# A new front for a fused attention and feed-forward kernel: log sums by a scan, zero matmuls ahead of the first scores, a first-layer group in quarters, and chunk 0's second layer by pairs of tiles

## The chip, the core and the metric

The kernel runs on one core of a Trainium2 chip. The metric is the device time of one execution in microseconds (us). Before the change the median of three runs is 324.0 us (323.47 to 324.17). Engines are named as in the profile: PE is TensorE (matmuls), PEld its weight loads, DVE is VectorE, ACT is ScalarE, POOL is GpSimd and SP is SyncE. Engines run side by side, each through its own instructions in order, and wait for one another by semaphores.

## The reference

```python
# attention with a forget gate; B=8, H=8, S=576, D=64
scores = (q @ k.T) / sqrt(D)
cum    = cumsum(log(clip(f, 1e-4, 1)))           # along the sequence
scores = where(causal, -1e9, scores + cum[:, None] - cum[None, :])
x      = softmax(scores) @ v                      # (B, H, S, D) -> (B*S, H*D) = (4608, 512)
# feed-forward
out    = gelu_tanh(x @ w_in) @ w_out              # w_in 512 x 2048, w_out 2048 x 512
```

## The kernel before

**Attention.** Four heads are one "quad", so there are 16 quads, two for each batch. `q` and `k` of a quad come by a casting DMA on POOL's queue and are put into column layout by a DVE transpose each (`TQ`, `TK`). Scores are computed with the keys on the partitions: a matmul with 32 rows per head, four heads side by side in four 32-row strips of the array (`S`; `H` does two heads only). ACT takes the exponential from PSUM into `pt` (line 285). The triangle at the diagonal is cut off afterwards, by POOL (`M`, line 291) or by DVE with a 0/1 mask (`m`, line 321). The decay needs no term in the scores: the factor exp(-cum - 64) of each key goes into the weights. `wT` holds it, `w_bf` is its bf16 copy, and `vw` is v times it (`vw` on DVE, `VW` on POOL). Denominators (`D`) and outputs (`V`) are matmuls with 32 columns per head, four heads side by side in four 32-column strips. DVE turns a denominator into a factor with transpose, reciprocal, transpose, and multiplies it into `xT` (line 379), which is the feed-forward input, transposed.

**Feed-forward.** Rows go in chunks of 512. The first layer multiplies `w_in` by `xT` with the whole array; ACT applies the gelu into `gT`. For chunk 0 it is done in halves of 256 rows and groups of four 128-wide blocks of d_ff: `J.half.group` (line 419). Groups with a capital J use the pool `psS` (two buffers of two PSUM banks, shared with the scores); those with a small j use the single tile of `psO`, shared with D and V. The second layer of chunk 0 (`mlp_out`, lines 658 to 674) computes four tiles of 128 rows, each as 16 "pulls" of 512 columns; a pull with the capital letter (`F.0.n`, n pulls) uses the whole array, one with the small letter (`f.0.n`) does the same in four strips of 32 columns. Later chunks use seven products in place of eight (`seven_products`, `F.c`/`f.c`, 256 columns a pull), with sums of the weights (`U`) and of the gelus (`G`) made on DVE.

**What sets the order.** The whole program is written out by hand in tables of words: `FRONT` up to the end of batch 3's attention and most of chunk 1's second layer, then `SECOND`, `STEADY` and so on, one word being one step. Each engine gets its instructions in the order of the words. So a step that waits holds up everything behind it on its engine. DMA words (`WI` and `WO` for the weights, `LQ`, `LK`, and `LP`, `LC` for v) stand in POOL's queue among the POOL masks; `LV` and the output stores stand in SP's.

**The front.** `setup` loads `f`, clips it (line 694) and takes its logarithm on ACT (695), transposes it on PE by five matmuls in FP32 into `ps_lt` (700), and ACT copies that to `logfT`. `CW` then makes the running sums on PE with FP32 matmuls against a triangle and a matrix of ones (719, 721), behind the first scores, and ACT turns them into `wT`. `B.n.c` are n matmuls of zeros with c columns (line 256) whose result nobody reads.

Of the kernel before, what the change touches and what calls it, by code (L numbers as in the profile page):

```python
# [16 lines left out]
def kernel(  # L17
# [194 lines left out]
    def transpose_words(src, dst):  # L212

        return nc.vector.transpose(  # L214
            out=dst.rearrange("p s c -> p (s c)").bitcast(FP32)
                .rearrange("p (t a) -> p a t", a=S // 32),
            in_=src.rearrange("p a d -> p (a d)").bitcast(FP32)
                .rearrange("p (a d) -> p a d", d=D // 2),
        )
# [33 lines left out]
    def keep_busy(n, cols=512):  # L253

        for _ in range(n):
            nc.tensor.matmul(idle_ps[0][:, 0:cols], idle[:, 0:128], idle[:, 0:cols],  # L256
                             start=True, stop=True)

# [146 lines left out]

    later = {}

    def mlp_in_half(half, g, spare=False):

        if spare:  # L410
            ph = psO.tile([128, 1024], FP32, name="ps_h", tag="po").rearrange("p (a n) -> p a n", n=512)
        else:
            ph = psS.tile([128, 2, 512], FP32, name="ps_h", tag="s")
        n0 = QA * half
        for dts in (range(N_DT - 1), range(N_DT - 1, N_DT)):
            for j in range(4):
                ft = 4 * g + j
                for dt in dts:
# [7 lines left out]
        later[half, g] = lambda: nc.scalar.activation(gT[:, 4 * g:4 * g + 4, n0:n0 + QA],  # L426
                             ph.rearrange("p a (b n) -> p (a b) n", n=QA), AF.Gelu_apprx_tanh)
        if not spare:
            later[half, g]()

# [227 lines left out]
    def mlp_out(c):  # L658

        for n in range(CH // 128):  # L660
            r0 = CH * c + 128 * n
            st = ostage_pool.tile([128, D_MODEL], FP32, name="o_st", tag="o")
            pso = psM.tile([128, D_MODEL], FP32, name="pso", tag="m")
            for ft in range(N_FT):
                cols = 32 if by_columns else 128
                for c0 in range(0, 128, cols):
                    nc.tensor.matmul(pso[c0:c0 + cols, :],  # L667
                                     gT[:, ft, 128 * n + c0:128 * n + c0 + cols],
                                     w_out_sb[:, ft, :],
                                     start=(ft == 0), stop=(ft == N_FT - 1), skip_group_check=True)  # L670
                if ft == N_FT - 1:
                    nc.vector.tensor_copy(st, pso)
                    nc.sync.dma_start(out=out[r0:r0 + 128, :], in_=st)
                yield


    def setup():
        nc.sync.dma_start(out=f_sb, in_=f.rearrange("b h s -> (b h) s"))
        dmas["LK.0"] = load_one(k, k_c, 0)
        dmas["LQ.0"] = load_one(q, q_c, 0)  # L680
        make_identity(nc, ident_f32)
        dmas["LK.1"] = load_one(k, k_c, 1)
        dmas["LQ.1"] = load_one(q, q_c, 1)
        make_upper_triangular(nc, utri_f32, val=1.0, diag=True)
# [9 lines left out]
        nc.vector.tensor_scalar(f_sb, f_sb, 1e-4, 1.0, op0=ALU.max, op1=ALU.min)
        nc.scalar.activation(f_sb, f_sb, AF.Ln)
# [20 lines left out]

    def make_w():
        cum_ps = psM.tile([128, NT * BH], FP32, name="cum_ps", tag="m")
        nc.tensor.matmul(cum_ps, utri_f32, logfT, start=True, stop=True)
# [34 lines left out]
    ops = {
        "W": lambda: cast_w(nc.vector.tensor_copy),
        "w": lambda: cast_w(nc.scalar.copy),
        "CW": make_w,
        "Z": zeros,
        "TR": lambda: triangles(nc.vector.tensor_copy),
# [99 lines left out]
```

## Time and profile before

| | us |
|---|---|
| median of three runs | 324.0 |
| the profiled execution, time | 323.22 |
| the profiled execution, span from first to last instruction | 321.4 |
| PE busy | 309.6 (96% of the span) |
| DVE busy | 242.0 (75%) |
| ACT busy | 212.7 (66%) |
| POOL busy | 107.8 (34%) |

The profile is of one execution. A row of a timeline gives the start, the length, the engine and line, the operation, the tile written and the tiles read, the shape and the count of instructions merged into it; in square brackets stands the idle time before it and what ended it. A matmul's end is modelled and lies past the start of the next one, so what a block of matmuls costs is read from its start to the start of the next block. A row of a list of waits gives the total, the number and the longest wait.

### The profile page before, as it was taken

The page shows a single profiled execution, that of the slowest core. Times are in us where ns is not written, and L with a number is a line of the kernel's source. Part 1 is how long each engine was busy: PE and PEld are TensorE (multiplying, and loading weights), DVE is VectorE, ACT ScalarE, POOL GpSimd, SP SyncE. Part 2 cuts the span into 40 slices and gives each one's busy share as a digit, 9 for nine tenths or more (in the row PEclk, how much of TensorE's full clock was granted, in tenths as well). Part 3 has the DMA queues.
Part 4 walks back from the last instruction along what each step waited for, and adds up shares of the span by engine and source line. Part 5 has one row for each costly group of instructions (what it writes and reads, how often), then busy time and mean ns, then how long its engine had stood idle before and what let it go on. Part 6 is the DMA issues. An engine that isn't in the chain of part 4 may idle for free.

```text
span 321.4 us, 11820 instructions
## 1 busy us (share of the span) xinstructions
PE 309.6 (96%) x5339; PEld 220.7 (69%) x5339; DVE 242.0 (75%) x374; ACT 212.7 (66%) x242; POOL 107.8 (34%) x145
## 2 busy tenths in 40 slices
PE   0899999999999999999999999999999999999996
PEld 0557844544776567776788878767776786688785
DVE  4765337898979879779877987699876866597674
ACT  4676576775766776878767866787586744836610
POOL 8989343522301416400851075205610140000000
PEclk9999999999999999999999999999999999999999
DMA  7999999585126931593139411971011111010203
GB/s 126 218 210 208 247 213 199 104 155 109 35 43 129 227 78 37 116 209 72 39 82 228 87 39 35 190 172 36 7 47 53 37 34 37 30 37 0 100 33 99
DMA packets 47490, 33.41 MB, mean 104 GB/s; under 512 B 29776, under 2 KB 42192, under 8 KB 47440
## 3 DMA queue, kind: packets, MB, share of 16 engines
q0 software_dynamic: 9632, 15.99, 28.3%
q1 hardware_dynamic: 37664, 16.60, 19.1%
q8 instruction: 41, 0.67, 0.9%
q14 instruction: 9, 0.07, 0.1%
q10 hardware_dynamic: 144, 0.07, 0.1%
HBM read 36.85 MB, written 9.44 MB: 144 GB/s over the span
## 4 chain that ended last, share of the span: by engine, by line
PE 91%; ACT 3%; DVE 3%; DMA 2%; issue 1%; POOL 0%; DVEq 0%; POOLq 0%
PE ps_w L600 30%; PE ps_h L395 19%; PE ps_s L277 9%; PE po L347 9%; PE ps_q L520 8%; PE pso L667 4%; PE ps_h L419 4%; PE ps_u L468 4%; DMA q_c<-in_q_dram 2%; PE po_m L333 1%; ACT pt L285 1%; ACT gT L403 1%; DVE xT L379 1%; PE idle_ps L256 1%; PE cum_ps L721 1%
## 5 line engine op out<-in xcount | busy, mean ns | idle before, releaser
L285 ACT ACTIVATE pt<-ps_s 128x1024 bf16<-128x1024 f32 (+2 forms) x100 | 94.0, 990 | 38.6 <-PE ps_s L277 35.9
L291 POOL TENSOR_SCALAR_AFFINE_SELECT pt<-pt 128x512 bf16<-128x512 bf16 (+3 forms) x65 | 41.4, 647 | 95.2 <-ACT pt L285 72.3
L395 PE MATMUL ps_h<-xT,w_in_sb 128*128 128x512 bf16 (+1 forms) x320 | 66.8, 358 | 0.3 <-ACT gT L403 0.2
L395 PEld LDWEIGHTS <-w_in_sb 128*128 128x128 bf16 x320 | 31.2, 98 | 26.6 <-issue 0.6
L600 PEld LDWEIGHTS <-gT 128*32 128x32 bf16 (+1 forms) x1216 | 44.1, 97 | 5.5 <-issue 2.2
L403 ACT ACTIVATE gT<-ps_h 128x1024 bf16<-128x1024 f32 x34 | 34.6, 1017 | 18.7 <-PE ps_h L395 18.4
L600 PE MATMUL ps_w<-w_out_sb,gT 128*32 128x256 bf16 (+1 forms) x1008 | 42.6, 273 | 0.0
L277 PE MATMUL ps_s<-qT,kT 32*128 32x64 bf16 (+5 forms) x896 | 36.3, 263 | 3.2 <-DVE qT L214 3.0
L600 PEld LDWEIGHTS <-gsum 128*32 128x32 bf16 (+1 forms) x948 | 35.4, 97 | 3.8 <-issue 1.5
L231 POOL TENSOR_TENSOR vw<-v_nat,wT 128x1280 bf16<-128x1280 f32 (+1 forms) x13 | 29.6, 2279 | 11.7 <-DMA v_nat<-in_v_dram 11.4
L536 DVE TENSOR_TENSOR usnap<-ps_q,usnap 128x1024 f32<-128x1024 f32 x15 | 17.9, 1222 | 18.6 <-PE ps_q L520 13.2
L277 PEld LDWEIGHTS <-kT 32*128 32x128 bf16 x896 | 16.5, 93 | 19.6 <-issue 10.1
L600 PE MATMUL ps_w<-usum,gsum 128*32 128x256 bf16 (+1 forms) x791 | 30.0, 273 | 0.0
L617 DVE COPY snap<-ps_w 128x512 f32<-128x512 f32 x32 | 21.8, 681 | 6.2 <-PE ps_w L600 6.0
L531 ACT ACTIVATE gT<-usnap 128x1024 bf16<-128x1024 f32 x15 | 15.8, 1054 | 12.1 <-DVE usnap L536 11.8
L379 DVE TENSOR_TENSOR xT<-po,rb 128x576 bf16<-128x576 f32 x26 | 19.5, 752 | 5.6 <-PE po L347 5.3
L347 PE MATMUL po<-pt,vw 128*32 128x64 bf16 (+4 forms) x624 | 22.4, 278 | 0.0
L214 DVE STREAM_TRANSPOSE qT<-q_c 128x576 f32<-128x576 f32 x16 | 19.8, 1246 | 1.7 <-DMA q_c<-in_q_dram 1.7
L347 PEld LDWEIGHTS <-vw 128*32 128x32 bf16 x672 | 14.6, 97 | 9.4 <-issue 2.8
L214 DVE STREAM_TRANSPOSE kT<-k_c 128x576 f32<-128x576 f32 x16 | 19.5, 1246 | 1.9 <-DMA k_c<-in_k_dram 1.9
L208 POOL DMA_DIRECT2D k_c<-in_k_dram x16 | 9.1, 568 | 33.6 <-DVE kT L214 18.0
L520 PEld LDWEIGHTS <-w_in_sb 128*128 128x128 bf16 x160 | 15.6, 98 | 2.5 <-issue 0.4
(135 smaller groups left out, 478.5 us busy)
## 6 DMA issues: line engine op xcount, KB each, us to landing
out_dram<-o_st SPq DMA_DIRECT2D x35, 256.0 KB, 2.3
k_c<-in_k_dram POOLq DMA_DIRECT2D x16, 288.0 KB, 5.3
q_c<-in_q_dram POOLq DMA_DIRECT2D x16, 288.0 KB, 6.3
v_nat<-in_v_dram SPq DMA_DIRECT2D x16, 256.0 KB, 5.4
v_nat<-in_v_dram SPq DMA_DIRECT2D x20, 128.0 KB, 5.1
v_nat<-in_v_dram POOLq DMA_DIRECT2D x8, 256.0 KB, 8.1
w_in_sb<-in_moe_w_in_dram POOLq DMA_DIRECT2D x8, 256.0 KB, 7.8
w_out_sb<-in_moe_w_out_dram POOLq DMA_DIRECT2D x4, 512.0 KB, 11.3
```

Source lines behind the costliest of these rows:

```text
L214: return nc.vector.transpose(out=dst.rearrange("p s c -> p (s c)").bitcast(FP32) .rearrange("p (t a) -> p a t", a=S // 32), in_=src.rearra ...
L231: return eng.tensor_mul(vw[i % 2][:, t0:t1], vb[:, t0:t1, h0:h0 + 4, :], wT[:, i, t0:t1, :].unsqueeze(3).to_broadcast([128, t1 - t0, 4, D]))
L277: nc.tensor.matmul(tiles[h // 2][:, h % 2, c0:c0 + nq], key_columns(i, key, h, c), qq[32 * h:32 * h + 32, q0:q0 + nq, c], start=(c == 0 an ...
L285: nc.scalar.activation(p[:, 2 * g:2 * g + 2, off:off + n], t[:, :, 0:n], AF.Exp, scale=scale)
L291: nc.gpsimd.affine_select(out=x, in_=x, compare_op=ALU.is_ge, fill=0.0, base=0, pattern=pattern, channel_multiplier=-1)
L347: nc.tensor.matmul(po[r0:r0 + w.shape[-1], 448 + q0:448 + q0 + nq], w, p[:, h, col:col + nq], start=(key in (0, "low")), stop=(key in ("lo ...
L379: nc.vector.tensor_mul(xT[:, 2 * u + x, r0 + s0:r0 + s1], po, rbs[i, part])
L395: nc.tensor.matmul(ph[:, j, n * cols:(n + 1) * cols], w_in_sb[:, dt, 128 * ft:128 * ft + 128], xT[:, dt, h0:h0 + cols], start=(dt == 0 and ...
L403: nc.scalar.activation(gelus(c, 2 * pr, 2), ph, AF.Gelu_apprx_tanh)
L520: nc.tensor.matmul(ps[:, k, HC * n:HC * n + HC], w[:, d, 128 * n:128 * n + 128], x[:, d, :], start=(first and n == 0 and d == 0), stop=(d ...
L600: nc.tensor.matmul(ps[c0:c0 + width, n, cols[0]:cols[1]], x[:, j, 128 * n + c0:128 * n + c0 + width], w[:, j, cols[0]:cols[1]], start=(fir ...
L617: copy(kept[name], ps)
```

## The change

- **Log sums.** The transposes of the logarithms, the copies to `logfT` and the FP32 matmuls go. DVE makes the running sum by one scan over the 576 columns (`SC`), PE transposes the sums (`CT`, five matmuls), and ACT makes `wT` from them in two parts (`CE.1`, then `CE.0` for the first two quads). `w_bf` is cast in two parts (`W.0`, `W.1`).
- **Zero matmuls.** 16 of them (7,808 columns) now stand ahead of the first scores, four of those held until the first `TK` (`BK` reads `kT`, and two plain ones are queued behind it); 16 (5,888 columns) stand behind. Before, ten (3,968 columns) stood behind the first scores.
- **Order of the front.** POOL's memsets (`zeros`) go to DVE. The first mask `M.0.0` now stands in POOL's queue ahead of six of the eight loads of `w_in`; before, five stood behind it. The triangle is made later on POOL (`UT`) and cast on ACT (`tr`). Two score rounds of four heads (`S.0.2`, `S.1.2`) become two rounds of two heads each.
- **A first-layer group in pieces.** Group 0 of half 0 is begun with four matmuls over the first quad's two blocks of `xT`, and ended with four and eight more; its sums are copied by DVE from `psO` into `u1` (`RJ`), which frees `psO` for group 1 (two pieces of eight matmuls). The gelu of group 0 is taken later from `u1`.
- **Chunk 0's second layer.** Two tiles of 128 rows are computed together, four pulls of the one and four of the other in turn, so that both buffers of `psM` are held and a quarter of `w_out` serves eight pulls.
- **Behind that**, plain and strip pulls, masks (more of them on POOL), `vw.5`, one sum of weights and the small copies `cl` are put elsewhere. The tables from `SECOND` on are the same, and both fronts end with 97 pulls of chunk 1 done.

```diff
     FRONT = """
-        Z TQ.0 LP.2 TR WI.1 TQ.1 S.0.0 B.1.384 CW WI.0 TK.1 S.0.2 LP.4 LP.3 B.1.512 vw.0.0 B.2.512 H.1.0.1 H.1.1.1 WI.3 M.0.0 W vw.1.0 WI.2 B.2.512
-        WI.5 LQ.2 WI.4 H.1.0.0 D.0.0 M.1.0.1 M.1.0.0 H.0.1.1 V.0.0.0 H.0.1.0 M.0.1 WI.6 V.0.1.0 B.2.256 H.1.1.0 B.1.256 D.1.0 H.0.3.0 B.1.256 V.1.0.0 H.0.3.1
-        WI.7 LK.2 V.1.1.0 m.0.3.2 H.1.3.0 j.0.0 vw.0.1 H.1.3.1 LC.1.4 WO.0 m.0.3.4 WO.1 D.0.1 M.1.3 S.1.2 M.1.1 VW.1.1 V.0.0.1 V.0.1.1 LC.1.2 D.1.1
-        J.0.1 J.0.2 WO.2 LC.1.0@VW.1.1 WO.3@m.0.3.2 V.1.0.1 V.1.1.1 LC.1.1 GJ.0.0 LC.1.3 TK.2 J.1.1 LK.3 J.0.3 J.1.0 LQ.3 TQ.2 LQ.4 VW.3
-        J.1.3 LK.4 J.1.2 F.0.4 X F.0.4 S.2.0 F.0.11 TK.3 S.2.2 F.0.6 LV.2.0 TQ.3 F.0.4 LK.5 S.2.1 F.0.2 F.0.7 TQ.4 m.2.1 S.3.0 vw.2 CL.2 M.2.2 f.0.7
-        M.2.0 D.2 S.3.1 f.0.7 LQ.5 V.2.0 m.3.0 S.3.2 TK.4 LK.6@LQ.4 f.0.1 f.0.3 V.2.1 M.3.2 f.0.2 S.4.1 CL.3 m.3.1 LQ.6 f.0.5 TQ.5 H.4.2.1 D.3 H.4.0.1
-        H.4.0.0 VW.4 V.3.1 v.3.0 f.0.1 H.4.2.0 U.0 m.4.1 LV.2.1@m.3.1 I.1.1 LQ.7@CL.3 I.1.4 TQ.6 I.1.6 m.4.2.3 I.1.0 m.4.2.2 I.1.5 CL.4 U.3 LV.3.0@LQ.7
+        LP.1 LP.4 SC LP.0 WI.0 B.8.512 B.1.512 CT TK.0 CE.1 TQ.0 CE.0 B.2.512 LP.3 B.1.128 BK.0.2 B.1.512 WI.5 B.1.512 S.0.0 TK.1 M.0.0 B.1.128
+        B.1.128 WI.1 WI.2 B.1.128 BK.0.1 B.3.512 H.0.2.1 B.1.128 BK.0.1 H.0.2.0 WI.3 H.0.1.0 W.0 LP.2 TQ.1 D.0.0 H.1.0.0 vw.0.0 B.1.128 B.2.512
+        BK.1.1 H.1.0.1 M.1.0 H.0.1.1 B.1.512 M.0.1 vw.1.0 V.0.1.0 B.1.128 B.1.512 V.0.0.0 H.0.3.0 UT D.1.0 j.0.0.4 V.1.0.0 V.1.1.0 H.1.3.1 WI.7 WI.4
+        H.0.3.1 WI.6 j.0.0.4 j.0.0.8 H.1.1.0 RJ.0.0 M.0.3 WO.0 H.1.1.1 vw.0.1 LC.1.1 D.0.1 j.0.1.8 H.1.3.0 M.1.1 WO.1 M.1.3 H.1.2.1 V.0.0.1 VW.1.1
+        V.0.1.1 UW.2.1 W.1 LQ.2 H.1.2.0 J.0.2 LK.2 LK.3 WO.2 D.1.1 j.0.1.8 GJ.0.1 V.1.0.1 V.1.1.1 TK.2 J.0.3 tr WO.3 J.1.1 TQ.2 GJ.0.0 LQ.3 U.0
+        J.1.3 J.1.2 J.1.0 F.0.1 f.0.3 LC.1.2 LC.1.0 f.0.2 S.2.0 TK.3 X f.0.2 PW.2.2 F.0.7 LC.1.3 F.0.1 S.2.2 f.0.2 F.0.1 TQ.3 f.0.2 LC.1.4 LQ.4 LK.5
+        f.0.4 S.2.1 F.0.1 f.0.4 LV.2.1 F.0.1 LK.4 F.0.3 M.2.2 F.0.1 vw.2 m.2.1 F.0.2 CL.2 LV.2.0 S.3.0 f.0.1 M.2.0 f.0.2 D.2 f.0.3 S.3.1 TQ.4 f.0.1
+        LQ.6 VW.3 f.0.4 M.3.0 f.0.1 V.2.0 TK.4 S.3.2 f.0.6 V.2.1 m.3.1 S.4.1 f.0.4 LQ.5 f.0.1 H.4.2.0 f.0.2 M.3.2 H.4.2.1 cl.3 D.3 VW.4 H.4.0.0
+        M.4.2.3 H.4.0.1 V.3.1 LK.6 v.3.0 f.0.1 F.0.1 I.1.2 I.1.0 TQ.5 U.1 TK.5 TQ.6 vw.5 I.1.5 UW.2.4 I.1.1 I.1.3 TK.6 U.3 I.1.4 U.2 m.4.2.2 I.1.6
...
+    def keep_busy_after(i, n):
+        for _ in range(n):
+            nc.tensor.matmul(idle_ps[0][:, 0:512], idle[:, 0:128], kT[i % 2][:, 64:64 + 256, :].rearrange("p s c -> p (s c)"),
+                             start=True, stop=True)
...
+    def keep_raw(half, g, copy):
+        raw = (u1, u2, u4)[len(raws)].rearrange("p f n -> p (f n)").bitcast(FP32).rearrange("p (b n) -> p b n", n=QA)
+        raws.append(raw)
+        copy(raw, held[half, g][0])
+        held[half, g][0] = raw
...
-        for dts in (range(N_DT - 1), range(N_DT - 1, N_DT)):
+        cut = 2 if spare else N_DT - 1
+        for dts in (range(cut), range(cut, N_DT)):
             for j in range(4):
...
-        for n in range(CH // 128):
-            r0 = CH * c + 128 * n
-            st = ostage_pool.tile([128, D_MODEL], FP32, name="o_st", tag="o")
-            pso = psM.tile([128, D_MODEL], FP32, name="pso", tag="m")
-            for ft in range(N_FT):
+        for pair in range(CH // 256):
+            psos = [psM.tile([128, D_MODEL], FP32, name="pso", tag="m") for _ in range(2)]
+            for part in range(4):
+                for n in range(2):
+                    r0 = CH * c + 256 * pair + 128 * n
+                    n0 = r0 - CH * c
+                    for ft in range(N_FT // 4 * part, N_FT // 4 * (part + 1)):
...
+    def running_sums():
+        nc.vector.tensor_tensor_scan(f_sb, ones_f32[0:BH, 0:1].to_broadcast([BH, S]), f_sb, 0.0,
+                                     op0=ALU.mult, op1=ALU.add)
...
-    def make_w():
-        cum_ps = psM.tile([128, NT * BH], FP32, name="cum_ps", tag="m")
-        nc.tensor.matmul(cum_ps, utri_f32, logfT, start=True, stop=True)
-        for n in range(NT - 1, 0, -1):
-            nc.tensor.matmul(cum_ps[:, n * BH:], ones_f32, logfT[:, :(NT - n) * BH], start=False, stop=True,
-                             skip_group_check=True)
+    def cum_tiles():
+        cums.append(psM.tile([128, NT * BH], FP32, name="cum_ps", tag="m"))
+        for t in range(NT):
+            n = min(128, S - 128 * t)
+            nc.tensor.transpose(cums[0][:n, t * BH:(t + 1) * BH], f_sb[:, 128 * t:128 * t + n], ident_f32)
...
```

More of the change, by code (lines that the diff above doesn't have):

```diff
@@ L425, in mlp_in_half @@
                     )
[L426 to L429, printed above, removed]
+                    if not spare and j == 3 and dt == N_DT - 1:
+                        later[half, g]()
+                    yield
     def x_block(c, b, t):
@@ L686, in setup @@
+        load_one(q, q_c, 1)
         nc.vector.memset(idle, 0.0)
         nc.vector.memset(ones_f32, 1.0)
-        nc.vector.memset(logfT, 0.0)
         nc.vector.memset(shift, -64.0)
@@ L754 @@
     ops = {
[L755 to L758, printed above, removed]
+        "W": lambda n: cast_w(nc.vector.tensor_copy, n),
+        "w": lambda n: cast_w(nc.scalar.copy, n),
         "TR": lambda: triangles(nc.vector.tensor_copy),
@@ L800 @@
         "B": keep_busy,
+        "BK": keep_busy_after,
         "X": load_exp,
```

99 lines of the change are left out of this document (54 added, 45 removed).

## The prediction

> **What bounds the kernel.** I read the page's chain that ended last first, then PE's waits up to 70 us, then the busy times by stage (the columns: length of the stage, then busy us and count of PE, PEld, DVE, ACT and POOL, PE's granted clock, DMA share and GB/s).
>
> ```profile
> PE 91%; ACT 3%; DVE 3%; DMA 2%; issue 1%; POOL 0%; DVEq 0%; POOLq 0%
> PE ps_s L277 <- DVE qT L214: 3.0, 1, 3.0
> PE ps_s L277 <- ACT pt L285: 0.2, 1, 0.2
> 8.62:40.66 32.04, 31.61 (x429) 22.33 (x429) 17.27 (x33) 21.61 (x26) 24.38 (x34) 1.00 1.17 222
> 40.66:98.93 58.27, 58.17 (x1059) 32.48 (x1056) 46.87 (x67) 41.43 (x44) 18.16 (x22) 1.00 0.58 116
> 98.93:321.40 222.47, 219.04 (x3857) 165.22 (x3849) 173.67 (x262) 145.89 (x168) 58.01 (x70) 1.00 0.35 83
> ```
>
> PE is the bound. It waits for the first scores until 8.62 and then for almost nothing. The stages are: 8.62 to 40.66, where chunk 0's second layer begins; 40.66 to 98.93, the end of the front; and the rest, whose order stays. In a stage where PE never rests, time is lost or won by what stands in its queue. So the sum is one of PE blocks, each from its start to the next start.
>
> **The start.** The first scores wait for `TQ.0`, and that for its load, which the change leaves second in POOL's queue.
>
> ```profile
> 3.58 0.45 DVE L694 TENSOR_SCALAR f_all<-f_all 64x576 f32<-64x576 f32 x1 [1.32 <-DMA f_all<-in_f_dram]
> 4.06 0.68 ACT L695 ACTIVATE f_all<-f_all 64x576 f32<-64x576 f32 x1 [1.97 <-DVE f_all L694]
> ...
> 5.89 1.26 DVE L214 STREAM_TRANSPOSE kT<-k_c 128x576 f32<-128x576 f32 x1 [1.86 <-DMA k_c<-in_k_dram]
> ...
> 7.30 1.26 DVE L214 STREAM_TRANSPOSE qT<-q_c 128x576 f32<-128x576 f32 x1 [0.15 <-DMA q_c<-in_q_dram]
> ```
>
> The scan is not in the trace. On DVE it stands between the logarithm's end (4.74) and `TK.0`. Its nearest row is the clip of the same tile, 0.45; the longest DVE row here is 1.26. It ends at 5.2 to 6.0, so `TK.0` moves by 0.1 at most and `TQ.0`, which waits for its load until 7.3, by 0.05. The five transposes (0.8 us before) and the four ACT instructions for `wT` then fit before 8.6. DVE takes over POOL's memsets during its 1.32 us wait for `f`. I take all this as 0, with the load as cover; without it each 0.1 us costs 0.1. First scores stay at 8.6.
>
> ```profile
> 8.62 0.83 PE L277 MATMUL ps_s<-qT,kT 32*128 32x256 bf16 x16 [2.96 <-DVE qT L214]
> 9.38 0.50 PE L256 MATMUL idle_ps<-idle 128*128 128x384 bf16 x1
> 9.67 1.27 PE L719 MATMUL cum_ps<-logfT,utri_f 128*128 128x320 f32 x2
> ...
> 12.52 0.46 PE L277 MATMUL ps_s<-qT,kT 32*128 32x320 bf16 x8
> 12.91 0.82 PE L256 MATMUL idle_ps<-idle 128*128 128x512 bf16 x3
> 13.93 1.22 PE L277 MATMUL ps_s<-qT,kT 32*128 32x256 bf16 x16 [0.20 <-ACT pt L285]
> 15.08 0.61 PE L256 MATMUL idle_ps<-idle 128*128 128x512 bf16 x2
> 15.62 0.51 PE L277 MATMUL ps_s<-qT,kT 32*128 32x256 bf16 x8
> 16.06 0.35 PE L333 MATMUL po_m<-pt,w_bf 128*32 128x256 bf16 x8
> ...
> 18.02 0.39 PE L256 MATMUL idle_ps<-idle 128*128 128x256 bf16 x2
> 18.34 0.63 PE L277 MATMUL ps_s<-qT,kT 32*128 32x320 bf16 x8
> ```
>
> **8.62 to 40.66, what goes.** (a) The running sums on PE: 9.67 to 12.52, 2.85 us. (b) The zero matmuls behind the first scores: 0.29 (9.38) and 1.02 (12.91, with a 0.20 wait), 0.54 (15.08, two of 512 columns), 0.32 (18.02, two of 256) and two single ones of 256 columns at 0.1 of columns and 0.1 of start each: 2.6 in all. (c) The first scores ran slowly, though the granted clock is given as 1.00 in every stage: 0.76 for 768 columns, and a zero matmul of 384 columns lasted 0.50, where three of 512 took 0.82 together at 12.91. At the later rate the scores cost 768 x 0.216/512 = 0.32 and a start of 0.13, so 0.45: 0.3 goes.
>
> **What comes.** (d) 5,888 zero columns in five blocks. At 0.216 us per 512 columns (below) that is 2.5, and the row at 18.02 shows 0.32 for 512 columns, 0.1 above that for a block's start: 3.0. (e) Two score rounds of four heads become pairs: at 12.52 four heads took 0.39, and two heads of 384 columns took 0.44 (15.62), so some 0.38 each at 320: +0.4 for both rounds. (f) The group in pieces gives three more starts of about 0.1: +0.25 for those. (g) New waits. The first exponentials (1.51 for both) now run from about 9.15 to 10.7, and `M.0.0`, two masks, takes 0.65 each by the page's mean or 0.9 as at its place before: it ends at 11.9 to 12.5.
>
> ```profile
> 9.47 1.51 ACT L285 ACTIVATE pt<-ps_s 128x768 bf16<-128x768 f32 x2 [2.00 <-PE ps_s L277]
> 12.76 1.77 POOL L291 TENSOR_SCALAR_AFFINE_SELECT pt<-pt 128x512 bf16<-128x512 bf16 x2
> ...
> L291 POOL TENSOR_SCALAR_AFFINE_SELECT pt<-pt 128x512 bf16<-128x512 bf16 (+3 forms) x65 | 41.4, 647 | 95.2 <-ACT pt L285 72.3
> ...
> 45.04 0.69 DVE L672 COPY o_st<-pso 128x512 f32<-128x512 f32 x1 [10.27 <-PE pso L667]
> ```
>
> PE reaches `D.0.0`, which needs it, at about 11.9. `M.1.0` ends at about 16.4, and PE is at `D.1.0` then. I take 0.3 for both, between 0 and 1.0: the wait is short if the mean holds. `RJ` copies 1,024 columns on DVE, some twice the 0.69; two score rounds and a D, 1.7 us on PE, lie over it, and each us beyond them would cost one. The sum: -2.85 - 2.6 - 0.3 + 3.0 + 0.4 + 0.25 + 0.3 = -1.8. Chunk 0's second layer would begin at 38.9.
>
> ```profile
> 40.66 1.89 PE L667 MATMUL pso<-w_out_sb,gT 128*128 128x512 bf16 x8
> 42.48 0.69 PE L277 MATMUL ps_s<-qT,kT 32*128 32x64 bf16 x24
> ...
> 45.59 0.63 PE L277 MATMUL ps_s<-qT,kT 32*128 32x320 bf16 x16
> 46.15 2.33 PE L667 MATMUL pso<-w_out_sb,gT 128*128 128x512 bf16 x10
> ...
> 51.70 1.69 PE L667 MATMUL pso<-w_out_sb,gT 128*32 128x512 bf16 x28
> 53.22 0.86 PE L347 MATMUL po<-pt,w_bf 128*32 128x512 bf16 x24
> 54.01 0.63 PE L277 MATMUL ps_s<-qT,kT 32*128 32x64 bf16 x16
> ...
> 66.25 13.97 PE L395 MATMUL ps_h<-xT,w_in_sb 128*128 128x512 bf16 x64
> 80.06 1.91 PE L600 MATMUL ps_w<-w_out_sb,gT 128*128 128x256 bf16 x16
> ...
> 98.82 2.03 PE L600 MATMUL ps_w<-w_out_sb,gsum 128*32 128x256 bf16 x19
> 100.69 0.59 PE L395 MATMUL ps_h<-xT,w_in_sb 128*128 128x512 bf16 x2
> ```
>
> **40.66 to 98.93.** The same matmuls in another order. 64 first-layer matmuls from 66.25 to 80.06 cost 0.216 each, and the step to the plain pulls behind them costs nothing. Eight pulls from 40.66 to 42.48 are 1.73 and 0.10 more; scores of 1,024 columns (0.43) took 0.56 from 45.59 to the next start, so 0.13 more. Seven strip pulls from 51.70 cost 7 x 0.217 and nothing on the way to D, which has the same strips; D (1,536 columns, 0.64) took 0.79 on the way to scores, 0.15 more. From 98.82 one strip pull (four of the 19 matmuls) and 15 plain ones of 256 columns, 16 x 0.108 = 1.73, took 1.87: 0.14 for the change from strips to plain. So a step costs 0.10 to 0.15 where the shape on the array changes (32-row strips, 32-column strips, whole) and nothing where it stays. [...]
>
> I count the changes of shape in the tables. Up to the second layer there are 29 before and 29 after. From there to the end of the front there are 33 before and 42 after, since plain and strip pulls of chunk 0 now alternate and single strip pulls stand between scores. Nine more at 0.135: +1.2. By a rule without that price it would be 0. Other costs there I set at nothing, and name what covers them: a pair of tiles needs both `psM` buffers, whose copy (0.69) fits under four pulls (0.86); the quarters of `w_out` arrive before their pulls; DVE loses masks to POOL and has `vw.5` in their place.
>
> **Sum.** -1.8 + 1.2 = -0.6. Against the profiled execution's own 323.22 that gives 322.6; its time lies 0.8 under the median of the runs, 324.0, so 323.4 for the median. About 0.2% (0.65 us) is what a measurement of this kernel can tell from no change, so the forecast lies just at that bound.
>
> **The rivals.** *The order costs nothing.* If the alternation of plain and strip pulls is hidden by weight loads, the 1.2 goes and the front's gain stays: 324.0 - 1.8 = 322.2, down to 321.6 if the waits of (g) are 0 and the shorter chain of DVE and ACT saves a few tenths. For it speaks that only one row shows the step from strip to plain pulls; against it that it costs the same as all the others.
>
> *Weights come late (slower).*
>
> ```profile
> w_in_sb<-in_moe_w_in_dram POOLq DMA_DIRECT2D x8, 256.0 KB, 7.8
> ...
> L197 POOL DMA_DIRECT2D w_in_sb<-in_moe_w_in_dram x8: 701/713/719, 9.1 to 20.3; - x8
> L185 POOL DMA_DIRECT2D v_nat<-in_v_dram x10: 708/915/952, 4.7 to 32.0; - x10
> DMA to landing us min/median/max: 6.7/7.8/9.0
> ```
>
> `M.0.0` waits on POOL for the first exponentials (10.7), and six loads of `w_in` stand behind it. Two masks, three loads of `w_in` and one of v (0.71 and 0.92 each to issue), three more masks, the triangle and `WI.7` put the issue of `WI.4` at about 18.8. At the median of 7.8 it lands at 26.6; PE reaches `J.0.2`, which needs it, at about 25.2, by 16.6 us of blocks behind 8.62 at the prices above: scores 6.9, D and V 3.5, pieces of the first layer 2.9, zeros 3.0, waits 0.3. PE would stand for 1.4, which gives -0.6 + 1.4 = +0.8: 324.8. At the minimum of 6.7 it is 0.3. It decides from a landing of about 26 us on. Against it: by then less is queued ahead of `WI.4` than before (`LQ.2` and its 288 KB now come later), and what took 7.8 us was mostly the queue.
>
> *PE is slow again at the first scores (slower).* The zero matmuls ahead of them end before 8.6 with gaps: nine from 1.3 us on, the transposes at about 6, then four from 7.2 on. Before, PE went over to the full rate at about 12, some 3 us into unbroken work from 8.62. If the gaps undo the effect, the scores (0.3) and the zero block of 2,432 columns (1.0) cost the old rate once more, and two score rounds 0.2: -0.6 + 1.5 = +0.9, so 324.9. [...]
>
> **Chances.** Forecast 0.42, with 322.5 to 324.3 as its own range (waits 0 to 1.0, the price of a change 0.10 to 0.15); it is half faster by over 0.2% and half within. The order free: 0.20, faster. Weights late: 0.20, slower but for 0.02. Slow first scores: 0.12, slower. Of the rest (0.06), waits in the later part of the front that nothing here shows, most is slower. So faster 0.42, same 0.24, slower 0.34. The range runs from 321.6, the first rival's lower end, to 325.2, the slow rivals with some of the waits of (g).
>
> **What would show it.** Right: the first scores still at about 8.6 and lasting 0.45; no rows of lines 719 and 721; chunk 0's second layer beginning at 38 to 40; the end of the front less than that stage's 58.3 us plus 1.5 later. Wrong: idle time ahead of `J.0.2` with a load of `w_in` as what ended it; a block of 512 zero columns at twice 0.22 behind the first scores; or strip and plain pulls that follow each other without the 0.14.

## The result: 1% slower, and the profile after

The changed kernel takes 327.31 us (median of six runs, 326.04 to 328.08) against 324.09 of the kernel before (323.47 to 324.75): a ratio of 1.0096, with a 95% interval of 1.0069 to 1.0123. The forecast was 323.4 with a range of 321.6 to 325.2, so it was wrong in size and in sign. The profiled execution took 326.98, with a span of 325.1, and stands 0.3 below the median.

The busy times by stage (columns as in the prediction). The stages are: first scores to chunk 0's second layer, that to the first layer of chunk 2, and the rest. Before, the middle one; the first is in the prediction and lasts 32.04, and the rest from 100.69 to 321.40 lasts 220.71:

```profile
40.66:100.69 60.03, 59.93 (x1075) 33.96 (x1073) 48.63 (x70) 43.17 (x45) 19.00 (x24) 1.00 0.59 119
```

After:

```profile
8.54:38.44 29.90, 28.92 (x423) 19.97 (x424) 19.30 (x33) 21.58 (x27) 24.61 (x36) 1.00 1.17 213
38.44:104.49 66.05, 62.40 (x1037) 34.14 (x1039) 46.52 (x65) 44.71 (x48) 20.89 (x30) 0.97 0.66 134
104.49:325.10 220.61, 216.46 (x3825) 163.63 (x3833) 170.80 (x255) 143.75 (x165) 56.77 (x68) 1.00 0.33 77
```

The first stage is 2.14 shorter, and it starts 0.08 earlier. The last is 0.10 shorter. The stage between them is 6.02 longer, and PE is idle in it for 3.65 where it was idle for 0.10; its granted clock is 0.97. So -0.08 - 2.14 + 6.02 - 0.10 = +3.7, the difference of the two spans. The whole loss lies between 38.44 and 104.49.

PE's waits after, three of those that the kernel before did not have (a fourth, of 1.3 ahead of the first zero matmul, delays nothing but zero matmuls):

```profile
PE po L352 <- DVE xT L384: 3.1, 1, 3.1
PE cum_ps L742 <- DVE f_all L721: 1.0, 1, 1.0
PE ps_h L436 <- DMA w_in_sb<-in_moe_w_in_dram: 0.4, 1, 0.4
```

The first is the loss. The timeline of PE around it (`V.5.0`, the output matmuls of half a quad, is the row at 99.77), then that of DVE:

```profile
96.34 0.29 PE L616 MATMUL ps_w<-usum,gT 128*32 128x256 bf16 x4
99.77 0.87 PE L352 MATMUL po<-pt,vw 128*32 128x512 bf16 x24 [3.14 <-DVE xT L384]
100.45 1.12 PE L616 MATMUL ps_w<-usum,gT 128*32 128x256 bf16 x17
101.36 3.29 PE L616 MATMUL ps_w<-w_out_sb,gsum 128*128 128x256 bf16 x16
104.49 1.89 PE L400 MATMUL ps_h<-xT,w_in_sb 128*128 128x512 bf16 x7
```

```profile
93.04 0.78 DVE L375 STREAM_TRANSPOSE rb<-rec 128x576 f32<-128x576 f32 x1
97.56 1.49 DVE L230 TENSOR_TENSOR vw<-v_nat,wT 128x1280 bf16<-128x1280 f32 x1 [3.74 <-ACT pt L290]
98.97 0.75 DVE L384 TENSOR_TENSOR xT<-po,rb 128x576 bf16<-128x576 f32 x1
```

`V.5.0` needs `psO`, the single buffer that `V.5.1` fills from 93.57 on. DVE frees it by `xT` (98.97). But `vw.6`, the product of v and the decay for the next batch, stands ahead of that `xT` in DVE's queue, and DVE stood still for 3.74 before it. The row names ACT as what ended the wait; the chain that ended last names another, in order of time:

```profile
91.73 5.65 DMA v_nat<-in_v_dram
...
98.97 0.76 DVE xT L384
...
99.77 0.87 PE po L352 x24
```

It is a load of v. SP's queue shows where the loads of v stood, first before, then after:

```profile
67.21 7.58 SPq L185 DMA_DIRECT2D v_nat<-in_v_dram  x10
...
98.63 3.75 SPq L185 DMA_DIRECT2D v_nat<-in_v_dram  x5
```

```profile
83.86 0.38 SPq L641 DMA_DIRECT2D out_dram<-o_st  x1
84.35 8.54 SPq L183 DMA_DIRECT2D v_nat<-in_v_dram  x10
```

The loads of v of batch 3 are `LV.3.0`, on which `vw.6` waits, and `LV.3.1`, which only the next quad needs, later; five loads each. By the tables, the ten at 67.21 before are `LV.2.1` and then `LV.3.0`, and the five at 98.63 are `LV.3.1`. The ten at 84.35 after are `LV.3.1` and then `LV.3.0`. So the change moved `LV.3.0` behind the store of chunk 1's first result, and put `LV.3.1`, which came some 14 us later before, in front of it. The last load of `LV.3.0` had been issued by 74.8 before; after, it is issued at 91.73 and has landed at 97.38. For `vw.6` the kernel before left some 23 us:

```profile
98.04 1.48 DVE L231 TENSOR_TENSOR vw<-v_nat,wT 128x1280 bf16<-128x1280 f32 x1
```

The wait is not the whole of it. The sixteen plain pulls of 256 columns at 101.36 last until 104.49, 0.196 each, where 0.108 is the rate before. In windows of PE's rest and of what follows, the granted clock falls:

```profile
96.45:99.77 3.32, 0.18 (x5) 0.00 (x0) 2.21 (x3) 3.29 (x4) 0.00 (x0) 1.00 0.05 11
99.77:104.60 4.83, 4.83 (x58) 3.35 (x58) 3.48 (x7) 0.12 (x1) 0.00 (x0) 0.65 0.29 99
```

So the theory taken to the chip was: late v loads hold DVE, DVE holds `psO`, PE rests 3.1 us and then runs nearly 4 us at about half its rate. The rival was that PE's own new order costs the time and the wait only shows it.

### The profile page after: what moved, and what is told of

Read it like the earlier page. It is cut to its first block, busy times and chain, and to the rows that moved or that the text cites. A ratio compares the mean times of both kernels' runs of the same rounds, so it can differ in the third digit from the quotient of the medians.

```text
span 325.1 us, 11762 instructions
## 1 busy us (share of the span) xinstructions
PE 313.9 (97%) x5301; PEld 220.0 (68%) x5318; DVE 242.9 (75%) x369; ACT 213.0 (66%) x246; POOL 109.6 (34%) x148
## 4 chain that ended last, share of the span: by engine, by line
PE 77%; DMA 6%; issue 6%; DVE 3%; ACT 3%; POOL 2%; SPq 2%; DVEq 0%; POOLq 0%
PE ps_w L616 27%; PE ps_h L400 14%; PE ps_q L536 8%; PE po L352 8%; PE ps_s L282 7%; PE pso L685 5%; PE ps_u L484 4%; PE ps_h L436 4%; DMA q_c<-in_q_dram 2%; DMA w_in_sb<-in_moe_w_in_dram 2%; SPq L183 2%; DMA v_nat<-in_v_dram 2%; POOL pt L296 1%; ACT pt L290 1%; DVE qT L213 1%
## 5 line engine op out<-in xcount | busy, mean ns | idle before, releaser
L296 POOL TENSOR_SCALAR_AFFINE_SELECT pt<-pt 128x512 bf16<-128x512 bf16 (+3 forms) x73 | 46.0, 640 | 96.7 <-ACT pt L290 73.8
L400 PE MATMUL ps_h<-xT,w_in_sb 128*128 128x512 bf16 (+1 forms) x308 | 65.6, 357 | 1.1 <-issue 0.3
L282 PE MATMUL ps_s<-qT,kT 32*128 32x64 bf16 (+5 forms) x896 | 35.4, 261 | 0.4 <-DVE qT L213 0.2
L230 POOL TENSOR_TENSOR vw<-v_nat,wT 128x1280 bf16<-128x1280 f32 (+1 forms) x12 | 27.3, 2276 | 0.8 <-DMA v_nat<-in_v_dram 0.5
```

Source lines behind the costliest of these rows:

```text
L230: return eng.tensor_mul(vw[i % 2][:, t0:t1], vb[:, t0:t1, h0:h0 + 4, :], wT[:, i, t0:t1, :].unsqueeze(3).to_broadcast([128, t1 - t0, 4, D]))
L282: nc.tensor.matmul(tiles[h // 2][:, h % 2, c0:c0 + nq], key_columns(i, key, h, c), qq[32 * h:32 * h + 32, q0:q0 + nq, c], start=(c == 0 an ...
L296: nc.gpsimd.affine_select(out=x, in_=x, compare_op=ALU.is_ge, fill=0.0, base=0, pattern=pattern, channel_multiplier=-1)
L400: nc.tensor.matmul(ph[:, j, n * cols:(n + 1) * cols], w_in_sb[:, dt, 128 * ft:128 * ft + 128], xT[:, dt, h0:h0 + cols], start=(dt == 0 and ...
```

## The experiments

The diffs of tables show only the words near a change, joined across the ends of lines.

**The two groups of loads swapped.**

```diff
-M.5.0 F.1.4 LV.3.1 F.1.5 S.5.1 D.4 F.1.5 LQ.8 F.1.2 LV.3.0 F.1.4
+M.5.0 F.1.4 LV.3.0 F.1.5 S.5.1 D.4 F.1.5 LQ.8 F.1.2 LV.3.1 F.1.4
```

> The two words LV.3.1 and LV.3.0 change places, nothing else. Theory A (one late load: vw.6 waits on DVE for the second of the two loads, the product into xT of V.5.1 stands behind it, and V.5.0 stands 3.1 us for it; then PE runs at half rate for some 3.5 us, which costs 1.7): the load that vw.6 needs is now issued first and lands at about 93.5, before DVE reaches vw.6, so both go: 327.3 - 4.8 = 322.5, idle PE ahead of V.5.0 under 0.3 us, granted clock 1.00 up to 110 us. Theory B (the new order of the whole front is slower by itself, the wait only takes slack that was lost elsewhere): 326 to 327.

Measured: 322.69 (10 runs), ratio 0.9959 (0.9938 to 0.9979). PE's timeline at the same place; the wait is gone, and the sixteen pulls run at 0.109:

```profile
96.14 0.85 PE L352 MATMUL po<-pt,vw 128*32 128x512 bf16 x24
97.48 1.91 PE L616 MATMUL ps_w<-w_out_sb,gsum 128*128 128x256 bf16 x16
99.22 1.89 PE L400 MATMUL ps_h<-xT,w_in_sb 128*128 128x512 bf16 x7
```

`LV.3.1` alone in the late place does no harm. Two words in other places take some 4.6 us off the changed kernel and make it faster than the one before. From `V.5.0` to the first layer it takes 3.08 here and 4.72 in the changed kernel, with the same matmuls: the lower rate costs 1.6, beside the 3.1 of the wait.

**The loads early**, both between the first layers of chunk 1, about where the kernel before had `LV.3.0`.

```diff
-f.0.1 F.0.1 I.1.2 I.1.0 TQ.5
+f.0.1 F.0.1 I.1.2 LV.3.0 LV.3.1 I.1.0 TQ.5
...
-M.5.0 F.1.4 LV.3.1 F.1.5 S.5.1 D.4 F.1.5 LQ.8 F.1.2 LV.3.0 F.1.4
+M.5.0 F.1.4 F.1.5 S.5.1 D.4 F.1.5 LQ.8 F.1.2 F.1.4
```

> Both loads of batch 3's v go to the beginning of chunk 1's first layer, about where they stood before. Theory A: as with the swap, 322.5, at most 0.2 us less, since nothing on DVE can wait for either load. Theory B: 326 to 327.

Measured: nine executions of 321.37 to 324.25, with a median of 323.07 and a ratio of 0.9966 (0.9938 to 0.9994), and one of 330.12 with a mean granted clock of 0.97. That is some 0.6 above the expected 322.5, and 3 to 4 below what the rival would give. The wait is gone here too.

**`vw.6` behind the `xT` that it held up**, the loads still late.

```diff
-S.6.1 vw.6 f.1.1 V.5.1 f.1.1 F.1.9 CL.6
+S.6.1 f.1.1 V.5.1 f.1.1 F.1.9 vw.6 CL.6
```

> The loads stay late, vw.6 moves on DVE behind the product into xT of V.5.1 and behind the copies of the fifth product. Theory A, which says that the place of the waiting instruction is what costs: V.5.0 no longer stands, but its own product into xT now waits behind vw.6 (97.5 to 99.0) and the next chunk's first layer for that, some 0.5 to 1 us: 322.8 to 323.6. If the late load costs wherever it is waited for, 326 to 327.

Measured: 323.93, ratio 0.9996 (0.9973 to 1.0019), a little above the 322.8 to 323.6 that were expected. The 3.1 us wait is gone, which shows that it goes through DVE's queue. Two new ones stand in the profile: 0.24 ahead of the first layer, for `xT`, and 1.00 within `V.5.1` that nothing in the profile explains:

```profile
95.37 0.64 PE L352 MATMUL po<-pt,vw 128*32 128x64 bf16 x17 [1.00 <-issue]
```

**The fault alone, put into the kernel before**: `LV.3.1` and then `LV.3.0` at 85.6, which puts `LV.3.0` later and `LV.3.1` earlier than it was, and `vw.6` ahead of `V.5.1`.

```diff
-CL.4 U.3 LV.3.0@LQ.7 U.1
+CL.4 U.3 U.1
...
-VW.5 M.5.0 f.1.13 S.5.2
+VW.5 M.5.0 LV.3.1 LV.3.0 f.1.13 S.5.2
...
-S.6.1 f.1.4 LK.7 V.5.1 f.1.3 f.1.10 vw.6 S.6.2 m.6.1 M.6.2.2 m.6.0 V.5.0 LV.3.1@LK.6 f.1.5
+S.6.1 vw.6 f.1.4 LK.7 V.5.1 f.1.3 f.1.10 S.6.2 m.6.1 M.6.2.2 m.6.0 V.5.0 f.1.5
```

> The kernel before with only this fault put in: both loads late (behind the first mask of quad 5) and vw.6 ahead of the product into xT of V.5.1. Theory A: a wait of 2 to 3 us ahead of V.5.0 and 1.5 of half rate, 324.1 + 3.5 to 4.8 = 327.6 to 328.9. Theory B: the old order has the slack for it, 324.1 to 325.

Measured: 324.68, ratio 1.0013 (0.9992 to 1.0034). A miss for the theory; the time is the one that the run's rival gave, an old order with slack for the fault. The theory as it stood was not the whole of it: late loads and the place of `vw.6` do next to nothing by themselves.

```profile
95.92 1.49 DVE L231 TENSOR_TENSOR vw<-v_nat,wT 128x1280 bf16<-128x1280 f32 x1
97.33 0.75 DVE L379 TENSOR_TENSOR xT<-po,rb 128x576 bf16<-128x576 f32 x1
```

```profile
98.14 0.87 PE L347 MATMUL po<-pt,vw 128*32 128x512 bf16 x24 [0.21 <-DVE xT L379]
```

The last load is issued at 92.02 here, later than in the changed kernel (91.73), yet `vw.6` starts at 95.92 and not at 97.56. And PE comes to `V.5.0` at 97.93 (98.14 less its wait), 1.3 later than the 96.63 of the changed kernel. These two, 1.6 and 1.3, are the 2.9 by which the wait is shorter. What made the loads land sooner? In the changed kernel POOL issues three loads of `q` and `k` (288 KB each) while SP issues those of v, at 85.72, 90.61 and 91.15; here there is only one, at 87.94.

**Those three loads moved behind `V.5.0`** in the changed kernel, the v loads left where they are.

```diff
-LQ.8 F.1.2 LV.3.0 F.1.4 S.5.2 V.4.0 f.1.1 M.5.1 M.5.2.2 M.5.2.3 LK.8 f.1.11 V.4.1 S.6.0 f.1.3 D.5 LQ.7@m.3.1 M.6.0
+F.1.2 LV.3.0 F.1.4 S.5.2 V.4.0 f.1.1 M.5.1 M.5.2.2 M.5.2.3 f.1.11 V.4.1 S.6.0 f.1.3 D.5 M.6.0
...
-S.6.2 m.6.2.3 f.1.1 V.5.0 f.1.4 F.1.2
+S.6.2 m.6.2.3 f.1.1 V.5.0 LQ.8 LK.8 LQ.7@m.3.1 f.1.4 F.1.2
```

> The changed kernel with the three loads of q and k that POOL issues among the v loads (at 85.72, 90.61 and 91.15) moved behind V.5.0; the v loads stay late. If these loads hold up the last v load, it lands about 1.5 us earlier (95.9 instead of 97.38), vw.6 ends at 96.4 instead of 99.0, PE's wait ahead of V.5.0 shrinks from 3.1 to 0.5 or less, the half rate behind it is gone, and the time is 322.5 to 323.5. If the last v load is late by itself, nothing changes: a wait of 3.1 and 327.3.

Measured: 322.79 (10 runs), ratio 0.9962 (0.9933 to 0.999). The view of the v loads between 83 and 100 us, the changed kernel and then this one (length of an issue in ns, minimum, median and maximum, first and last start; then issue to landing in us):

```profile
L183 SPq DMA_DIRECT2D v_nat<-in_v_dram x10: 409/602/1542, 84.4 to 91.7; - x10
...
DMA to landing us min/median/max: 3.7/5.0/6.5
```

```profile
L183 SPq DMA_DIRECT2D v_nat<-in_v_dram x10: 417/532/1551, 84.1 to 90.3; - x10
...
DMA to landing us min/median/max: 2.5/3.7/4.1
```

DVE's timeline here:

```profile
93.96 1.49 DVE L230 TENSOR_TENSOR vw<-v_nat,wT 128x1280 bf16<-128x1280 f32 x1 [0.36 <-DMA v_nat<-in_v_dram]
95.37 0.75 DVE L384 TENSOR_TENSOR xT<-po,rb 128x576 bf16<-128x576 f32 x1
```

Without the three, the last load is issued 1.4 earlier and the loads land 1.3 sooner at the median; `vw.6` starts 3.6 earlier, which is all of PE's wait. I had expected the landing 1.5 earlier; it came more than 3 earlier, since the issue on SP speeds up too. The other profiles agree: where the same three loads stand among the ten of v, the median from issue to landing is 4.7 (the swap), 5.4 (`vw.6` late) and 5.0 (the changed kernel); with the one load in the kernel before with the fault it is 4.3, and without any 3.7. So three things had to come together: `LV.3.0` late, other loads among the loads of v, and `vw.6` ahead of the `xT` that PE needs. Each of the three undone takes the wait away.

**Zero matmuls in the wait**: the changed kernel with nine matmuls of 512 zero columns, in a `psS` tile, ahead of `V.5.0`.

```diff
-S.6.2 m.6.2.3 f.1.1 V.5.0
+S.6.2 m.6.2.3 f.1.1 ZS.9 V.5.0
...
+    def zeros_in_scores(n):
+        ps = psS.tile([128, 2, 512], FP32, name="ps_z", tag="s")
+        for _ in range(n):
+            nc.tensor.matmul(ps[:, 0, :], idle[:, 0:128], idle, start=True, stop=True)
```

> The changed kernel as it is, with nine zero matmuls of 512 columns (1.9 us) put into the wait ahead of V.5.0, into a buffer of the scores that comes free at about 97.4. The wait stays 3.1 us from the last strip pull to V.5.0. If the half rate behind it comes from PE's rest, it goes, and with it 1.7: 325.6, the sixteen plain pulls at 0.108 in place of 0.205. If it has another cause, 327.3.

Measured: 326.7 (4 runs), ratio 1.0084 (1.006 to 1.0108). That is a miss on the time: 1.6 should have come back, and 1.0084 can't be told from the changed kernel's 1.0096 (1.0069 to 1.0123).

```profile
97.34 2.10 PE L262 MATMUL ps_z<-idle 128*128 128x512 bf16 x9 [0.89 <-ACT pt L296]
101.12 0.87 PE L358 MATMUL po<-pt,vw 128*32 128x512 bf16 x24 [1.68 <-DVE xT L390]
102.48 1.91 PE L622 MATMUL ps_w<-w_out_sb,gsum 128*128 128x256 bf16 x16
104.23 1.89 PE L406 MATMUL ps_h<-xT,w_in_sb 128*128 128x512 bf16 x8
```

That the lower rate comes with the unbroken rest is shown all the same: with the rest broken into 0.89 and 1.68, the sixteen pulls run at 0.109 again, and from `V.5.0` to the first layer it takes 3.11. The mean granted clock of a whole execution says so beyond this one profile: it is 0.990 to 0.995 in all six executions of the changed kernel and 1.000 in all four here. But `V.5.0` came at 101.12 in this execution, 1.35 later than in the changed kernel's, so that the wait itself was longer and ate the gain: by the chain of that profile, the last v load was issued at 92.12 and landed at 98.74. Why it took longer there was not followed up.

**Fewer changes of shape**: the version with early loads, with 19 pulls of chunk 0 made plain and 22 of chunk 1 made strips, so that the shape on the array changes 34 times between chunk 0's second layer and the end of the front, and not 42.

```diff
-F.0.1 f.0.3 LC.1.2 LC.1.0 f.0.2 S.2.0 TK.3 X f.0.2 PW.2.2 F.0.7 LC.1.3 F.0.1 S.2.2 f.0.2 F.0.1 TQ.3 f.0.2 LC.1.4 LQ.4 LK.5 f.0.4 S.2.1 F.0.1 f.0.4
+F.0.1 F.0.3 LC.1.2 LC.1.0 F.0.2 S.2.0 TK.3 X F.0.2 PW.2.2 F.0.7 LC.1.3 F.0.1 S.2.2 F.0.2 F.0.1 TQ.3 F.0.2 LC.1.4 LQ.4 LK.5 F.0.4 S.2.1 F.0.1 F.0.4
...
-D.4 F.1.5 LQ.8 F.1.2 F.1.4 S.5.2
+D.4 f.1.5 LQ.8 f.1.2 f.1.4 S.5.2
...
-V.5.1 f.1.1 F.1.9 CL.6 M.6.1 F.1.2 S.6.2
+V.5.1 f.1.1 f.1.9 CL.6 M.6.1 f.1.2 S.6.2
```

> The kernel with the loads early, and 14 pulls of chunk 0 made plain, 22 of chunk 1 made strips, so that changes of shape in the later front fall from 42 to 34. By the price of the prediction, 0.135 each: 1.1 less than with the loads early alone (322.5), so 321.4. By the rival that the order of shapes is free: the same as with the loads early.

Measured: 321.34 (320.65 to 322.85, six runs), ratio 0.9923 (0.9897 to 0.995): the fastest version of all, faster than both kernels. The middle stage, in the kernel with the three loads moved (with the loads early it lasts 61.10 too) and then in this one:

```profile
38.23:99.33 61.10, 61.10 (x1042) 33.27 (x1039) 47.17 (x65) 44.36 (x47) 21.12 (x30) 1.00 0.62 129
```

```profile
39.73:100.28 60.55, 60.55 (x1051) 33.99 (x1048) 47.03 (x65) 44.37 (x47) 21.36 (x30) 1.00 0.71 145
```

Eight changes fewer, 0.55 us less: 0.07 each, half of the prediction's price. The time came as expected (321.4), but that is 1.7 under the version with early loads, of which this stage gives a third; what gave the rest is open, as executions of one version lie 2 to 3 us apart. The profiled execution was the slowest of the six, and shows something else at the start:

```profile
6.59 0.49 PE L742 MATMUL cum_ps<-ident_f,f_all 64*128 64x64 f32 x5 [1.69 <-DVE f_all L721]
7.01 0.66 PE L255 MATMUL idle_ps<-idle 128*128 128x512 bf16 x3
7.64 0.90 PE L261 MATMUL idle_ps<-kT,idle 128*128 128x512 bf16 x2
9.33 0.83 PE L282 MATMUL ps_s<-qT,kT 32*128 32x256 bf16 x16
```

After a rest of 1.69, the transposes and three zero matmuls still run at the full rate (0.49 and 0.66); then PE runs slowly from about 7.7 to 10.8 (granted clock 0.53 between 7.60 and 10.80), the first scores take 0.76 to the next start and begin 0.8 later than in the changed kernel, and chunk 0's second layer begins at 39.73. The words up to there are the changed kernel's own, so it is the execution that differs. Three runs ask what the zero matmuls do there.

**No zero matmuls ahead of the first scores** (the version with early loads).

```diff
-LP.0 WI.0 B.8.512 B.1.512 CT TK.0 CE.1 TQ.0 CE.0 B.2.512 LP.3 B.1.128 BK.0.2 B.1.512 WI.5 B.1.512 S.0.0
+LP.0 WI.0 CT TK.0 CE.1 TQ.0 CE.0 LP.3 WI.5 S.0.0
```

> The kernel with the loads early, without the sixteen zero matmuls ahead of the first scores. If they are what makes PE run at the full rate from the first scores on, PE is slow until about 12: first scores 0.76 in place of 0.45 and the zero block behind them 2.0 in place of 1.0, in all 0.5 to 1.5 more: 323.0 to 324.0. If PE's waits for ACT cover that, or the rate was full anyway: 322.5.

Measured: its ten executions fall into two groups, four of 322.63 to 323.21 (whose ratio is 0.9972, 0.995 to 0.9993) and six of 328.9 to 329.99; the profile is of the second group. There PE works without a rest from 8.41 on and runs at about half its rate for some 20 us:

```profile
24.78 2.74 PE L436 MATMUL ps_h<-xT,w_in_sb 128*128 128x256 bf16 x12
...
32.35 1.92 PE L436 MATMUL ps_h<-xT,w_in_sb 128*128 128x256 bf16 x16
```

Twelve matmuls of 256 columns take 2.68 to the next start (0.22 each) at 24.78; sixteen take 1.85 (0.12) at 32.35. So leaving the zero matmuls out costs nothing in some executions and 6 us in others; I had expected 0, or 0.5 to 1.5. With them, one execution of ten was that long too (the 330.12 with the loads early).

**More of them** (12 for 9 ahead of the five transposes), in the version with fewer changes of shape.

```diff
-WI.0 B.8.512 B.1.512 CT
+WI.0 B.11.512 B.1.512 CT
```

> The version with early v loads and fewer changes of shape, with 12 instead of 9 zero matmuls from 1.3 us on, so that PE's pause ahead of the five transposes (1.0 to 1.7 us, by when the scan ends) is filled. If that pause decides whether the first scores run slowly, every execution begins at the full rate: first scores 0.45 to 0.52 in the profile, a spread under 1 us instead of 2.2, and a median of 321.0 (between 320.6 and 321.3). If it doesn't matter, or if the zero matmuls end later than the scan, 321.3 to 321.8 with the same spread.

Measured: 321.94 (321.34 to 323.0), ratio 0.9934 (0.9908 to 0.996). The rest ahead of the transposes is filled in the profile and the first scores begin at 8.44, but the median is not lower than with nine, and the spread hardly smaller (1.7 against 2.2). A miss: what makes one execution 1 to 2 us longer than another is not that rest alone. Its middle stage is 60.56, as with nine, which repeats the 0.55.

**Fewer of them** (5 for 9), in the same version.

```diff
-WI.0 B.8.512 B.1.512 CT
+WI.0 B.4.512 B.1.512 CT
```

> The same version with 5 instead of 9 zero matmuls from 1.3 us on, so that PE rests some 2.9 us ahead of the five transposes. If the pause decides, the first scores run at the old rate in every execution (0.76) and the full rate comes at about 11 to 12: 322.5 to 323, and up to 329 if the half rate then lasts as it did without any zero matmuls. If what counts is only the zero matmuls from 7 us on, 321.3.

Measured: 325.85 (324.63 to 328.55, ten runs), ratio 1.0069 (1.0042 to 1.0095); no execution is as fast as the slowest with nine.

```profile
6.25 0.77 PE L742 MATMUL cum_ps<-ident_f,f_all 64*128 64x64 f32 x5 [2.68 <-DVE f_all L721]
6.95 1.14 PE L255 MATMUL idle_ps<-idle 128*128 128x512 bf16 x3
...
9.73 0.62 PE L282 MATMUL ps_s<-qT,kT 32*128 32x256 bf16 x16
...
97.15 1.27 PE L616 MATMUL ps_w<-usum,gT 128*32 128x256 bf16 x37 [1.57 <-issue]
```

After a rest of 2.68 the transposes take 0.77 for 0.49 and three zero matmuls 1.14 for 0.66, and since the scores stand behind them they begin 1.3 later than with twelve (8.44). The rate had not come up before the rest either: the five zero matmuls from 1.26 on last 2.31, 0.46 each. So this run shows a full rate that comes late, at about 10 us, and not one that a rest undid. The scores begin 1.3 later than without any zero matmuls, too (8.41): at the low rate the zero matmuls ahead of them are a delay. The direction was as expected; the time lies between the two sizes named (322.5 to 323, up to 329). In the profiled execution, against the one with twelve, chunk 0's second layer begins only 0.54 later, and the middle stage is 2.50 longer (63.06 for 60.56). Of that, 1.57 is a stop ahead of 97.15 which nothing in the profile explains. It looks like the 1.00 with `vw.6` late. Its cause stays open, and so does the rest of the 2.50.

## Why the prediction was wrong, point by point

**The start: right, by its cover.** The scan took 1.35, beyond the longest row of 1.26, and ran from 4.81 to 6.16, past the forecast's 6.0. `TK.0`, which it was to delay by 0.1 at most, moved by 0.2, from 5.89 to 6.09, but `TQ.0` from 7.30 to 7.23, and the first scores start at 8.54:

```profile
4.81 1.35 DVE L721 TENSOR_TENSOR_SCAN f_all<-ones_f,f_all 64x576 f32<-64x576 f32 x1 [0.75 <-ACT f_all L718]
...
7.23 1.26 DVE L213 STREAM_TRANSPOSE qT<-q_c 128x576 f32<-128x576 f32 x1
8.54 0.52 PE L282 MATMUL ps_s<-qT,kT 32*128 32x256 bf16 x16 [0.16 <-DVE qT L213]
```

The load of q was the cover, as said. The scan's 1.35 is three times the clip of the same tile (0.45), which the prediction took as its nearest row, and 1.8 times a product of two FP32 operands over as many columns (0.75, line 384).

**The front stage: right, a little better.** -1.8 was forecast, and -2.14 came; chunk 0's second layer begins at 38.44, against 38.9. The first scores are at the full rate (0.46 to the next start), as step (c) has it. The waits of step (g) did not come from the masks: the one wait that the profile records in this stage is 0.37 ahead of `J.0.2`, for `w_in`. That is the rival "weights come late" in small, at its lower end of 0.3.

**The order of the middle: right in its sum, the price open.** Nine more changes of shape at 0.135 were to cost 1.2. Without the stall the stage takes 61.10 against 60.03: +1.07. That is the sum over everything in the stage; eight changes taken out again gave 0.55 and not 1.1, so part of the 1.07 is something else, or the price differs from change to change.

**The failed step: "Other costs there I set at nothing".** The three covers that it names hold: no wait for them is in the profile. The list was what failed: it named what the edit of `mlp_out` touches and the masks, and neither `LV.3.0` on SP's queue nor `vw.6` on DVE was in it, though the tables move both. The list under "The change" leaves them out as well, and its diff ends before these lines. Two steps that the prediction did not cost gave 3.14 of wait and 1.6 of lower rate, 4.8 in all (the stage grew by 6.02; with 1.07 of order, 0.2 stays unassigned). The prediction had "waits in the later part of the front that nothing here shows" at 0.06. The risk could be seen, if not its size: in the trace before, SP has issued the last load of `LV.3.0` by 74.8, and `vw.6` starts at 98.04, 23 us later; the new tables put `LV.3.0` behind a store and behind `LV.3.1`, with loads of `q` and `k` between. With the stall away the spans fall to 319.8 (the swap) and 319.9 (the three loads later) from 321.4, and the ratios to 0.996. The stages give -2.2 + 1.07 = -1.1 us and the spans -1.5, where the prediction's sum had -0.6.

**The lower rate after the wait** was weighed for the first scores alone, as the third rival, with a chance of 0.12. How long a rest on PE brings it on was not shown: the trace before has only the way up to the full rate, at about 12. Here a recorded rest of 3.14 was followed by a granted clock of 0.65. In the changed kernel's profile the first scores are not slow, after a rest of 1.03. In the profile of the version with fewer changes of shape, which has the same words up to there, they were, after a rest of 1.69, and chunk 0's second layer began 1.3 later than in the changed kernel, close to the 1.5 of that rival. So the rival did come about in an execution with the same words, and it was luck that it did not in the changed kernel's profiled one.

## What to carry to other kernels

Where a program is written out as queues, list every word that changes its place on every queue, and look up for each load how long before its use it is issued and lands: a load that moves from 23 us ahead of its use to 6 us can become a wait where it takes that long to land (here 5.65). A step that waits for a load must not stand in front of a step that frees a buffer for the bounding engine (here 3.14 us of wait on PE, gone with `vw.6` behind the `xT`). And a stall on TensorE is to be priced with the slower matmuls behind it, where the trace shows them: here 1.6 us behind the 3.14, half as much again.

## What the runs showed of the hardware

- A rest of 3.14 us on PE was followed by matmuls at 0.196 per 256 columns for 0.108, from about 0.7 us behind the rest to about 104.5, nearly 4 us: 1.6 us lost. Rests of 0.89 and 1.68 with 2 us of zero matmuls between were followed by none of it.
- A rest of 1.69 us, with only 3.6 us of work before it, was once followed by the same, 1.0 us after its end (granted clock 0.53 for some 3 us). So the length of the rest alone doesn't decide.
- With no zero matmuls ahead, six of ten executions took some 6 us longer than the other four. The one profiled, of the six, ran at about half the rate for some 20 us of work without a rest. The granted clock is given as 1.00 through it: there the durations of the rows tell (0.22 for a matmul of 256 columns at 24.78, 0.12 at 32.35) and the clock doesn't.

```profile
8.41:28.00 19.59, 19.59 (x172) 8.57 (x175) 7.94 (x16) 8.90 (x11) 11.18 (x19) 1.00 1.02 181
```

- Three loads of 288 KB on POOL's queue made ten v loads on SP's queue both slower to issue (84.1 to 90.3 became 84.4 to 91.7) and slower to land (a median of 3.7 became 5.0, and 4.7 to 5.4 in three further profiles).
